# Taking the steps of a fused convolution and MLP in pairs: both first products, then both second products

## The chip, the cores and the metric

The kernel runs on one core of a Trainium2 chip. The metric is the device time of one execution in microseconds; the time of the kernel before is the median of three runs. The profile is that of one further execution.

## The reference

```
w = softmax(weight)                       # 8 heads x 7 taps
x_unf = x_pad[:, idx, :]                  # the last 7 rows of the sequence, zeros ahead of it
out = einsum('hk,bskhg->bshg', w, x_unf)  # causal convolution; 192 channels, 24 to a head
h = out.reshape(B * S, D) @ w_in          # 32768 x 192 by 192 x 2048
g = h * (1.0 / (1.0 + np.exp(-1.702 * h)))
return g @ w_out                          # by 2048 x 192
```

Everything is float32, with B = 8, S = 4096 and D = 192.

## The kernel before

**Tiling.** The work is cut into 32 "big" pieces of 1024 tokens of x (two batches of 512 tokens), and each into two steps, an even and an odd one: 64 steps. Within a step, the first product (by `w_in`, L463) gives eight tiles of hidden values, 128 partitions x 1024 each; ScalarE's gelu (L479) writes them to `g`; the second product (by `w_out`, `product2`, L553, and `quarters`, L569) gives the 192 outputs of the step's tokens.

**Fewer multiplications.** Both products are done in a scheme that saves block products and pays with sums of blocks. For the first, `terms` runs through 21 terms, each a call of `product1`: four pairs of matmuls, one half of the array's rows reading `f` and the other `crossed`. Their results are gathered in four PSUM tiles (`slots[0]` to `slots[2]`, called x, y and z in turn, and `sums`), and in five SBUF tiles `kept` (k15, k20, k19, k18, k16), by copies on ScalarE and additions on VectorE. For the second, `g` holds the four plain tiles B11, B12, B21, B22 and three sums, T1 = B12 - B11, T2 = B22 - T1 and T4 = T2 - B21; T3 = B22 - B12 takes B12's place. Each is in two halves of 128 x 1024 (u = 0, 1), and `sum_g` (L489) makes one half of one sum on VectorE.

**Steps.** The first two steps (`first_step`, `second_step`) use plain products, because the sums of weights aren't there yet. Then, for each step, `hidden` does the 21 terms, and `output` the five `product2` (p1, p2, p6, p5, p7) and the quarters. So TensorE alternates in each step between two shapes of matmul: 64 rows x 128 columns (L463) and 128 rows x 32 columns (L553, L569). Near its end, `hidden` calls `fetch`, which starts term 16 of the next step in a free slot, and `begin` copies the result to `sums`.

**What sets the order.** The schedule is written by hand: each engine runs its instructions in the order of the program, and the framework adds the waits on semaphores. Term 3 and term 19 near the end of `hidden` add to `sums` after k20's addition (L533) has read it. In `output`, T4 is read by the fourth column group of p5, and p2 reads B21.

**Work for the next x.** `prepare(big)` makes a list, `todo`, of VectorE instructions: three transposes of x, 21 taps of the convolution (L402, L404), eight sums of blocks, and DMAs that cross halves of `f` to the other partitions (`cross`). `work(us)` takes as many from the list as fit into the given time by fixed costs (0.76 for a tap, 0.7 for a transpose) and puts them at this place of VectorE's order. `need` takes all up to a label.

**Output.** `output` keeps partial sums u1, u2, p3, p4 in SBUF, adds to them on VectorE, transposes (`turn`, L587) into `osb`, and SP stores it.

The lines that set a step of `hidden` and its successors, where the change acts:

```
pe(sums, 1, 9, first=True)
pe(y, 15)
sum_g(0, T1)
work(1.1)
vec.tensor_add(k20, k20, sums)
...
sum_g(0, T2)
fetch()
pe(sums, 3, 19)
```

Of the kernel before, what the change touches and what calls it, by code (L numbers as in the profile page):

```python
# [8 lines left out]
F32 = mybir.dt.float32  # L9
U32 = mybir.dt.uint32  # L10
# [5 lines left out]
def kernel(  # L16
# [7 lines left out]
):  # L24

# [25 lines left out]
    P = 128  # L51
# [28 lines left out]
    u_pool = ctx.enter_context(tc.tile_pool(name="u", bufs=1))  # L80
    osb_pool = ctx.enter_context(tc.tile_pool(name="osb", bufs=2))
# [34 lines left out]
    NS = 7  # L116
    B11, B12, B21, B22, T1, T2, T4 = range(NS)
    T3 = B12
    g = consts.tile([P, NS, NK, T], F32)

# [44 lines left out]
    FREE = 10  # L165

# [6 lines left out]
    kept = [consts.tile([P, 2, TOK], F32, name=f"kept{i}") for i in range(5)]  # L173

# [10 lines left out]
    assert PIECE == CW * D and NW * 2 * PIECE == 3 * NK * T and 3 * PIECE <= NB * T  # L188
    raw = g[:, T1 : T4 + 1, :, :].rearrange("p s f t -> p (s f t)").bitcast(U32)
    raw = raw.rearrange("p (i n) -> p i n", i=NW)  # L190

    assert 2 * K * R <= NK * T and PIECE <= 2 * TOK and 3 * PIECE <= 2 * NJ * XW
    diag = g[:, B22, :, :].rearrange("p f t -> p (f t)")[:, 0 : 2 * K * R]
    diag = diag.rearrange("p (c k q) -> p c k q", c=2, k=K)

    def scratch(flat):
# [5 lines left out]
        [k.rearrange("p h n -> p (h n)")[:, 0:PIECE].bitcast(U32) for k in kept[0:3]],  # L202
# [4 lines left out]
    SET = (0, 1, 2, 0, 1, 3, 0, 1)  # L207
# [4 lines left out]
    ident = consts.tile([P, P], F32)  # L212
# [11 lines left out]
    for i in range(NW):  # L224
        piece = raw[:, i, :].rearrange("p (k f) -> p k f", k=NC)
        for h in range(2):
            nc.sync.dma_start(out=piece[halves[h], :, :], in_=w_in_v[i // 2, i % 2, h])


    sel = consts.tile([H, NC, P], F32)  # L230
# [13 lines left out]

    fold = consts.tile([P, R], F32)
# [6 lines left out]
    def words(i):  # L252
        w = raw[:, i % NW, :].rearrange("p (n w) -> p n w", w=2)
        return (w[:, :, 0], w[:, :, 1]) + tuple(sets[SET[i]])

# [67 lines left out]
    def load_w_out(i):  # L323
        nc.sync.dma_start(
            out=raw[:, i, :].rearrange("p (c d) -> p c d", c=CW),
            in_=w_out_v[:, i * CW : (i + 1) * CW, :],
        )
# [149 lines left out]
    def gelu(b, u, src):  # L477
        j = NK // 2 * u
        act.activation(  # L479
            g[:, b, j : j + NK // 2, :].rearrange("p f t -> p (f t)"),  # L480
            src.rearrange("p h n -> p (h n)"),
            AF.Gelu_apprx_sigmoid,
        )

    def sum_g(u, dst):
        j = NK // 2 * u
        v = [g[:, b, j : j + NK // 2, :] for b in range(NS)]
        a, b = {T1: (B12, B11), T2: (B22, T1), T3: (B22, B12), T4: (T2, B21)}[dst]
        vec.tensor_sub(v[dst], v[a], v[b])  # L489
# [6 lines left out]
    def hidden(s, x, z, y, work, fetch):  # L496

        k15, k16, k19, k18, k20 = kept

        def pe(slot, *ts, first=False):  # L500
            terms(s, slot, *ts, first=first)

        pe(sums, 12)
        act.copy(k15, sums)
        pe(x, 5, 17)
        gelu(B11, 0, x)
        pe(z, 7, first=True)
        pe(sums, 0)
        act.copy(k16, sums)
        work(1.5)  # L510
        pe(y, 6, 14, first=True)
        vec.tensor_sub(x, z, k15)
        work(2.6)
        pe(sums, 13)
        act.copy(k19, sums)  # L515
        pe(x, 2)
        act.copy(k18, x)
        pe(z, 11)
        pe(sums, 20, 10)
        vec.tensor_sub(k15, y, k19)  # L520
        gelu(B12, 0, sums)
        pe(x, 4)
        act.copy(k20, x)
        vec.tensor_sub(k19, z, k19)
        work(1.1)
        gelu(B22, 1, k19)
        gelu(B22, 0, k15)
        pe(y, 8)
        pe(sums, 1, 9, first=True)
        pe(y, 15)  # L530
        sum_g(0, T1)
        work(1.1)
        vec.tensor_add(k20, k20, sums)  # L533
        vec.tensor_sub(k16, y, k16)
        gelu(B11, 1, k20)
        pe(x, 18)
        gelu(B21, 1, x)
        gelu(B21, 0, k16)
        sum_g(0, T2)
        fetch()  # L540
        pe(sums, 3, 19)
        work(0.7)
        vec.tensor_add(k18, k18, sums)  # L543
        gelu(B12, 1, k18)
        work(1.1)

    def product2(slot, bank, ab, last, first=True):

        dst = slot[:, bank, 0:T]
        tiles = [(c, *ab, c) for c in range(NC)] + [(NC, *last)]  # L550
        for j in range(NK):
            for l, a, b, c in tiles:
                nc.tensor.matmul(  # L553
                    dst[l * Q : (l + 1) * Q, :],
                    w_out_s[:, a, j, c * Q : (c + 1) * Q],
                    g[:, b, j, :],
                    start=(first and j == 0),
                    stop=(j == NK - 1),
                    skip_group_check=True,
                )  # L560
        return dst[0 : NC * Q, :], dst[NC * Q :, :]

    def quarters(slot, bank, a, b, c):

        dst = [slot[l * Q : (l + 1) * Q, bank, 0:T] for l in range(4)]
        for i in range(NK // 4):
            for l in range(4):
# [4 lines left out]
                    g[:, b, j, :],  # L572
# [6 lines left out]
    class Out:  # L579


        def __init__(self, s):
            self.s = s
            self.osb = osb_pool.tile([NC * Q, 2, T // Q, 2 * Q], F32, name="osb")
# [24 lines left out]
    def output(s, ra, rb, work, between=None):  # L609

        out = Out(s)
        u1, u2, p3, p4 = (
            u_pool.tile([NC * Q, T], F32, name=f"u{i}") for i in range(4)
        )

        p1, p3c = product2(ra, 0, (A11, B11), (S4, B22, 0))
        act.copy(u1, p1)
        act.copy(chunk(p3, 0), p3c)
        sum_g(1, T1)
        sum_g(1, T2)  # L620
        sum_g(1, T4)
        sum_g(0, T4)
        p2, p3c = product2(rb, 0, (A12, B21), (S4, B22, 1))
# [3 lines left out]
        sum_g(0, T3)  # L627
        sum_g(1, T3)
        p6, p3c = product2(ra, 1, (S2, T2), (S4, B22, 2))
        act.copy(chunk(p3, 2), p3c)  # L630
        vec.tensor_add(u2, u1, p6)
        work(4.2)
        if between:
            between()
        p5, p4c = product2(rb, 1, (S1, T1), (A22, T4, 0))
        q = quarters(rb, 0, A22, T4, 2)
# [4 lines left out]
        out.turn(0, 1, p3)  # L641
        for l in (0, 1, 3):
            vec.tensor_add(chunk(p4, 2), chunk(p4, 2), q[l])
        work(1.5)
        p7, p4c = product2(ra, 0, (S3, T3), (A22, T4, 1))
# [42 lines left out]
    def first_step():  # L688
# [53 lines left out]
        gelu(B11, 0, slots[0])  # L742
        gelu(B12, 0, sums)
        for m, n, slot, b in quarters[2:]:
            plain(0, 0, m, n, slot)
            gelu(b, 0, slot)
# [11 lines left out]
        split_piece(5)  # L758
        split_rest(5)
        round_w_out(0)  # L760
        round_w_out(1)
        split_piece(6)
        split_piece(7)
        for m, n, slot, b in quarters:
            plain(0, 1, m, n, slot)
            gelu(b, 1, slot)
        split_rest(6)
        split_rest(7)
        round_w_out(2)
        round_w_out(3)  # L770


        todo.extend(prepare(1))
        todo.extend(("", 0.42, lambda i=i: sums_w_in(i)) for i in range(FREE))
        out = Out(0)
        c22 = u_pool.tile([NC * Q, T], F32, name="u0")
        quarter = [(0, 0), (0, 1), (1, 0)]
        for k in range(2):
            for i, (m, n) in enumerate(quarter):
                c, c22c = product2(  # L780
                    slots[i % 2],
# [5 lines left out]
                if k == 1:  # L787
                    work((6.0, 0.7, 2.3)[i])
                    out.turn(m, n, c)
                    act.copy(chunk(c22, i), c22c)  # L790
                    if i == 0:
                        sums_w_out()
        out.turn(1, 1, c22)
        out.store()

    def second_step(fetch):

        quarters = [
            (0, 0, slots[2], B11), (1, 0, sums, B21), (1, 1, slots[0], B22), (0, 1, slots[1], B12)
        ]  # L800
        for u in range(2):
            for i, (m, n, slot, b) in enumerate(quarters):
                plain(1, u, m, n, slot)
                gelu(b, u, slot)
                if u == 1 and i < 2:
                    sum_g(0, (T1, T2)[i])
                work(2.5)
        todo.extend(("", 0.42, lambda i=i: sums_w_in(i)) for i in range(FREE, len(SUMS_W)))
        todo.append(("sums", 0.0, lambda: None))
        todo.extend(prepare(2))  # L810
        output(1, slots[0], slots[1], work, fetch)
        need("all 1")
        cross(1, 1)
        need("sums")

    first_step()
    y, x, z = slots[0], slots[2], slots[1]
# [6 lines left out]
    def begin(slot):  # L824
        act.copy(sums, slot)

    def fetch_2():
        fetch(2, x)
        begin(x)

    second_step(fetch_2)
    for s in range(2, N_ST):
        more = s + 1 < N_ST
        hidden(s, x, z, y, work, lambda: fetch(s + 1, z) if more else None)
        give(s)
        if more:
            begin(z)
# [37 lines left out]
```

## Time and profile before

| | |
|---|---|
| runs (us) | 2381.71, 2382.17, 2382.23 |
| median | 2382.17 |
| span of the profiled execution | 2380.2 |
| TensorE matmuls / VectorE / ScalarE busy | 2370.6 / 2038.6 / 1055.7 |
| granted TensorE clock | 1.00 |
| repeat of a step in the middle | 36.60 |
| VectorE busy in two steps of 36.60 (985.37 to 1058.57) | 34.07 and 29.41 |

In a line of groups stand the source line, the engine, the operation, what it writes and reads, partitions x elements and type, and the count; then the busy time in us and the mean of one in ns; then the engine's idle time just ahead of such instructions, and what ended most of it. In a timeline, the first column is the start in us from the start of the span, the second the time from the first start to the last end of the instructions merged into that line, and a bracket gives idle time before it and who ended it. "PE" is the matmul, "PEld" the load of its weights, "DVE" is VectorE and "ACT" ScalarE. An fp32 matmul shows as two instructions, so that the page counts twice as many as the program has.

### The profile page before, as it was taken

Reading aid. Unit: us, or ns where it says so; the run is one execution under the profiler, and the core shown is the slowest. Engines: PE = TensorE matmul, PEld = TensorE weight load, DVE = VectorE, ACT = ScalarE, POOL = GpSimd, SP = SyncE. Lnnn points to the kernel's source line nnn. Section 1 sums busy time; section 2 is a strip of 40 time slices with the busy share of each in tenths; the row PEclk is TensorE's granted clock in tenths of the full one; section 3 lists DMA queues with packets and bytes.
Section 4 is the critical chain, followed back from the end, with each engine's and each line's share of the span. In section 5 each row is a group of like instructions: output and inputs, shape, how many; then the busy total and the mean of one; then the engine's idle time right before and its main releaser. Section 6 shows DMA issues by size and latency. Waiting matters only on the chain.

```text
span 2380.2 us, 71629 instructions
## 1 busy us (share of the span) xinstructions
PE 2370.6 (100%) x32602; PEld 1749.3 (73%) x32602; DVE 2038.6 (86%) x2853; ACT 1055.7 (44%) x1369; POOL 9.1 (0%) x30
## 2 busy tenths in 40 slices
PE   9999999999999999999999999999999999999998
PEld 7777777777777777777777777777777777777776
DVE  8898988888888889888898888898888988889865
ACT  6345344344453443444534434445344344453443
POOL 1000000000000000000000000000000000000000
PEclk9999999999999999999999999999999999999999
DMA  7322323223233132331232321323313233123120
GB/s 164 72 50 56 66 52 66 49 42 68 50 68 59 30 68 56 63 65 36 55 68 51 66 51 40 69 50 67 59 30 68 58 61 66 39 53 68 25 42 15
DMA packets 195823, 135.89 MB, mean 57 GB/s; under 512 B 110752, under 2 KB 186016, under 8 KB 193536
## 3 DMA queue, kind: packets, MB, share of 16 engines
q1 hardware_dynamic: 194912, 131.06, 28.1%
q8 instruction: 255, 4.18, 0.7%
q14 instruction: 48, 0.39, 0.1%
q10 hardware_dynamic: 560, 0.13, 0.0%
q0 software_dynamic: 48, 0.13, 0.0%
HBM read 53.15 MB, written 25.17 MB: 33 GB/s over the span
## 4 chain that ended last, share of the span: by engine, by line
PE 99%; ACT 0%; DVE 0%; POOL 0%; issue 0%; POOLq 0%
PE slot L553 47%; PE slot L463 28%; PE sums L463 21%; PE slot L569 2%; PE slot L675 1%; ACT g L479 0%; POOL sel L235 0%; PE sums L366 0%; PE slot L377 0%; DVE w_in_s L295 0%; DVE f L291 0%; ACT xin L281 0%; ACT xin L280 0%; ACT f L281 0%; ACT f L282 0%
## 5 line engine op out<-in xcount | busy, mean ns | idle before, releaser
L553 PE MATMUL slot<-g,w_out_s 128*32 128x256 f32 x20544 | 1133.5, 379 | 0.0
L553 PEld LDWEIGHTS slot<-g,w_out_s 128*32 128x32 f32 x20544 | 661.0, 110 | 451.2 <-issue 20.9
L463 PE MATMUL slot<-f,w_in_s 64*128 64x256 f32 x3120 | 724.7, 376 | 1.6 <-DVE w_in_s L295 1.6
L463 PE MATMUL slot<-crossed,w_in_s 64*128 64x256 f32 x3120 | 724.7, 376 | 0.0
L489 DVE TENSOR_TENSOR g<-g 128x1024 f32<-128x1024 f32 x504 | 602.7, 1216 | 81.8 <-ACT g L479 76.7
L463 PEld LDWEIGHTS slot<-f,w_in_s 64*128 64x128 f32 x3120 | 583.1, 187 | 36.8 <-ACT kept L278 2.0
L463 PEld LDWEIGHTS slot<-crossed,w_in_s 64*128 64x128 f32 x3120 | 583.1, 187 | 34.9 <-issue 0.4
L463 PE MATMUL sums<-f,w_in_s 64*128 64x256 f32 x2280 | 558.9, 379 | 0.0
L463 PE MATMUL sums<-crossed,w_in_s 64*128 64x256 f32 x2280 | 558.9, 379 | 0.0
L463 PEld LDWEIGHTS sums<-crossed,w_in_s 64*128 64x128 f32 x2280 | 421.4, 187 | 36.7 <-issue 12.8
L463 PEld LDWEIGHTS sums<-f,w_in_s 64*128 64x128 f32 x2280 | 421.4, 187 | 36.7 <-issue 12.8
L404 DVE SCALAR_TENSOR_TENSOR f<-xt,cw,f 128x512 f32<-128x512 f32 (+1 forms) x570 | 423.1, 742 | 14.4
L479 ACT ACTIVATE g<-kept 128x1024 f32<-128x1024 f32 x310 | 320.9, 1058 | 141.6 <-DVE kept L543 82.5
L479 ACT ACTIVATE g<-slot 128x1024 f32<-128x1024 f32 x136 | 138.3, 1017 | 49.2 <-PE slot L463 49.2
L637 ACT COPY u<-slot 32x256 f32<-32x256 f32 x63 | 23.1, 367 | 248.5 <-PE slot L569 248.5
L520 DVE TENSOR_TENSOR kept<-slot,kept 128x1024 f32<-128x1024 f32 x62 | 75.7, 1221 | 63.7 <-ACT kept L515 63.7
L533 DVE TENSOR_TENSOR kept<-kept,sums 128x1024 f32<-128x1024 f32 x62 | 75.7, 1221 | 55.9 <-PE sums L463 55.9
L587 DVE STREAM_TRANSPOSE osb<-u 96x256 f32<-96x256 f32 x253 | 111.2, 439 | 7.1 <-ACT u L790 0.4
L479 ACT ACTIVATE g<-sums 128x1024 f32<-128x1024 f32 x66 | 67.5, 1023 | 97.8 <-PE sums L463 97.8
L630 ACT COPY u<-slot 32x256 f32<-32x256 f32 x63 | 23.0, 364 | 194.5 <-PE slot L553 194.5
L515 ACT COPY kept<-sums 128x1024 f32<-128x1024 f32 x62 | 62.7, 1012 | 97.8 <-PE sums L463 97.8
L543 DVE TENSOR_TENSOR kept<-kept,sums 128x1024 f32<-128x1024 f32 x62 | 75.7, 1221 | 27.2 <-PE sums L463 24.3
(116 smaller groups left out, 1353.3 us busy)
## 6 DMA issues: line engine op xcount, KB each, us to landing
xin<-in_x_dram SPq DMA_DIRECT2D x240, 180.0 KB, 5.0
crossed<-f SPq DMA_DIRECT2D x31, 832.0 KB, 5.7
out_dram<-osb SPq DMA_DIRECT2D x382, 64.0 KB, 1.9
crossed<-f SPq DMA_DIRECT2D x31, 448.0 KB, 3.8
crossed<-f SPq DMA_DIRECT2D x31, 256.0 KB, 2.9
crossed<-f SPq DMA_DIRECT2D x31, 128.0 KB, 2.2
g<-in_moe_w_in_dram SPq DMA_DIRECT2D x8, 384.0 KB, 9.8
g<-in_moe_w_out_dram SPq DMA_DIRECT2D x4, 768.0 KB, 4.8
```

The source lines that it names most:

```text
L404: vec.scalar_tensor_tensor(out=dst, in0=src, scalar=tap, in1=dst, op0=ALU.mult, op1=ALU.add)
L463: nc.tensor.matmul(slot[:, h, j * T : (j + 1) * T], w_in_s[halves[h], a, j * P : (j + 1) * P], (f if h == o else crossed)[halves[h], b, :] ...
L479: act.activation(g[:, b, j : j + NK // 2, :].rearrange("p f t -> p (f t)"), src.rearrange("p h n -> p (h n)"), AF.Gelu_apprx_sigmoid,)
L489: vec.tensor_sub(v[dst], v[a], v[b])
L515: act.copy(k19, sums)
L520: vec.tensor_sub(k15, y, k19)
L533: vec.tensor_add(k20, k20, sums)
L543: vec.tensor_add(k18, k18, sums)
L553: nc.tensor.matmul(dst[l * Q : (l + 1) * Q, :], w_out_s[:, a, j, c * Q : (c + 1) * Q], g[:, b, j, :], start=(first and j == 0), stop=(j == ...
L569: nc.tensor.matmul(dst[l], w_out_s[:, a, j, c * Q : (c + 1) * Q], g[:, b, j, :], start=(i == 0), stop=(i == NK // 4 - 1), skip_group_check ...
L587: vec.transpose(self.osb[:, n, :, m * Q : (m + 1) * Q], src.rearrange("p (j t) -> p j t", t=Q),)
L675: nc.tensor.matmul(slots[c][halves[h], 0 if h == o else 1, n * T : (n + 1) * T], diag[halves[o], c - 1, k, :], xts[0][halves[o], c, n, Q - ...
```

## The change

The steps of a big piece are run as a pair: `hidden` of the even step, `hidden` of the odd one, then `output` of the even step and `output` of the odd one. What has to live longer, or in another place, follows from that:

- `g` holds the four plain tiles twice, one set for each step of a pair. T4 is written into B21's place.
- The five kept tiles become one tile, `room`. T1 and T2 of the step whose output is being made lie in k15, k20, k19 and k18, and u1, u2, p3, p4 in k16.
- In the odd `hidden`, T1 and T2 (half 0) of the even step are made; the odd step's follow in the even `output`, behind the additions to p4. Term 7 comes first in the odd `hidden`, since its slot is free. The even `hidden` copies the fetched slot to y, which serves the odd step as `sums`.
- In `output` T3 comes ahead of T4, and the amounts of `work` change.
- The first two steps are merged (`first_steps`): their first products all come ahead of their second ones. The loaded words of the weights, `ident`, `sel`, `fold` and `diag` get other places.

```diff
-    g = consts.tile([P, NS, NK, T], F32)
+    T3, T4 = B12, B21
+    g = consts.tile([P, 2, NU, 4, NK // NU, T], F32)
+    room = consts.tile([P, 5, 2 * TOK], F32)
+    k15, k20, k19, k18, k16 = (room[:, i, :].rearrange("p (h n) -> p h n", h=2) for i in range(5))
+    us = [room[0 : NC * Q, 4, i * T : (i + 1) * T] for i in range(4)]
+    def half(s, b, u):
+        if b in (T1, T2):
+            return room[:, 2 * (b - T1) + u, :].rearrange("p (f t) -> p f t", t=T)
+        return g[:, s % 2, u, b, :, :]
...
-    def hidden(s, x, z, y, work, fetch):
+    def hidden(s, x, z, y, sums, work, fetch):
+        if second:
+            pe(z, 7, first=True)
         pe(sums, 12)
         act.copy(k15, sums)
         pe(x, 5, 17)
-        gelu(B11, 0, x)
-        pe(z, 7, first=True)
+        gelu(s, B11, 0, x)
+        if not second:
+            pe(z, 7, first=True)
         pe(sums, 0)
         act.copy(k16, sums)
-        work(1.5)
+        work(3.2 if second else 1.5)
...
         pe(y, 15)
-        sum_g(0, T1)
+        if second:
+            sum_1(s - 1, 0)
+        else:
+            work(1.2)
         work(1.1)
         vec.tensor_add(k20, k20, sums)
         vec.tensor_sub(k16, y, k16)
-        gelu(B11, 1, k20)
+        gelu(s, B11, 1, k20)
         pe(x, 18)
-        gelu(B21, 1, x)
-        gelu(B21, 0, k16)
-        sum_g(0, T2)
+        gelu(s, B21, 1, x)
         fetch()
+        if not second:
+            act.copy(y, z)
+        gelu(s, B21, 0, k16)
+        if second:
+            sum_2(s - 1, 0)
+        else:
+            work(1.2)
         pe(sums, 3, 19)
...
     def output(s, ra, rb, work, between=None):
-        sum_g(1, T1)
-        sum_g(1, T2)
-        sum_g(1, T4)
-        sum_g(0, T4)
+        sum_1(s, 1)
+        sum_2(s, 1)
+        sum_3(s, 0)
+        sum_3(s, 1)
+        work(0.7)
...
         out.turn(0, 0, u2)
-        sum_g(0, T3)
-        sum_g(1, T3)
+        sum_4(s, 0)
+        sum_4(s, 1)
...
-        work(4.2)
+        work(3.2)
...
-        out.turn(0, 1, p3)
         for l in (0, 1, 3):
             vec.tensor_add(chunk(p4, 2), chunk(p4, 2), q[l])
-        work(1.5)
+        out.turn(0, 1, p3)
+        if s % 2:
+            work(1.5)
+        else:
+            sum_1(s + 1, 0)
+            sum_2(s + 1, 0)
...
-    for s in range(2, N_ST):
-        more = s + 1 < N_ST
-        hidden(s, x, z, y, work, lambda: fetch(s + 1, z) if more else None)
-        give(s)
-        if more:
-            begin(z)
-        if s % 2 and (s + 3) // 2 < N_BIG:
-            todo.extend(prepare((s + 3) // 2))
-        output(s, y, x, work)
-        if s % 2 and more:
-            need(f"all {(s + 1) // 2}")
-            cross((s + 1) // 2, 1)
-        x, z = z, x
+    for big in range(1, N_BIG):
+        s = 2 * big
+        more = big + 1 < N_BIG
+        hidden(s, x, z, y, sums, work, lambda: fetch(s + 1, z))
+        give(s)
+        x, z, y, sums = z, x, sums, y
+        hidden(s + 1, x, z, y, sums, work, lambda: fetch(s + 2, z) if more else None)
+        if more:
+            act.copy(sums, z)
+        output(s, y, x, work)
+        if more:
+            need(f"all {big + 1}")
+            cross(big + 1, 1)
+        if big + 2 < N_BIG:
+            todo.extend(prepare(big + 2))
+        output(s + 1, x, y, work)
+        x, y, z = z, x, y
```

More of the change, by code (lines that the diff above doesn't have):

```diff
@@ L79 @@
     f_pool = ctx.enter_context(tc.tile_pool(name="f", bufs=2))
-    u_pool = ctx.enter_context(tc.tile_pool(name="u", bufs=1))
-    osb_pool = ctx.enter_context(tc.tile_pool(name="osb", bufs=2))
     psum = ctx.enter_context(tc.tile_pool(name="psum", bufs=1, space=bass.MemoryType.PSUM))
@@ L112 @@
     sums = psum.tile([P, 2, TOK], F32, name="sums")
-    NS = 7
-    B11, B12, B21, B22, T1, T2, T4 = range(NS)
-    T3 = B12
-    g = consts.tile([P, NS, NK, T], F32)
+    B11, B12, B21, B22, T1, T2 = range(6)
+    T3, T4 = B12, B21
[3 more added lines that the diff above has]
+    us = [room[0 : NC * Q, 4, i * T : (i + 1) * T] for i in range(4)]
+    osbs = consts.tile([P, 2, 2 * TOK], F32)
+    def half(s, b, u):
+        if b in (T1, T2):
+            return room[:, 2 * (b - T1) + u, :].rearrange("p (f t) -> p f t", t=T)
+        return g[:, s % 2, u, b, :, :]
     NB = 13
@@ L163 @@
     ]
-    FREE = 10
     TERMS = [
@@ L170 @@
     ]
-    kept = [consts.tile([P, 2, TOK], F32, name=f"kept{i}") for i in range(5)]
+    NS = 7
     A11, A12, A21, A22, S1, S2, S4 = range(NS)
@@ L187 @@
     PIECE = NC * UW
[L188 to L194, printed above, removed]
+    assert PIECE == CW * D and 3 * PIECE <= NB * T and 3 * PIECE <= 2 * NJ * XW
+    flat_room = room.rearrange("p i n -> p (i n)")
+    flat_osb = osbs.rearrange("p i n -> p (i n)")
+    later = [g[:, 1, u, :, :, :].rearrange("p b f t -> p (b f t)") for u in range(NU)]
+    at = [(flat_osb, 0), (flat_room, 3 * PIECE), (later[1], 2 * TOK), (later[1], 2 * TOK + 2 * PIECE)]
+    assert 5 * PIECE + R <= 4 * 2 * TOK and 2 * TOK + 4 * PIECE <= 4 * NK // NU * T
+    raw = [t[:, i : i + 2 * PIECE].bitcast(U32) for t, i in at]
+    diag = later[0][:, 0 : 2 * K * R].rearrange("p (c k q) -> p c k q", c=2, k=K)
+    sel = flat_osb[0:H, 2 * PIECE : 2 * PIECE + NC * P].rearrange("i (c q) -> i c q", c=NC)
+    ident = flat_osb[:, 2 * PIECE + NC * P :]
+    assert 2 * PIECE + (NC + 1) * P == 4 * TOK
+    fold = flat_room[:, 5 * PIECE : 5 * PIECE + R]
     def scratch(flat):
@@ L201 @@
         scratch(tmp),
-        [k.rearrange("p h n -> p (h n)")[:, 0:PIECE].bitcast(U32) for k in kept[0:3]],
+        scratch(flat_room),
         None,
@@ L205 @@
     ]
-    SET = (0, 1, 2, 0, 1, 3, 0, 1)
+    SET = (0, 1, 2, 0, 1, 3, 1, 3)
     w8 = consts.tile([H, K], F32)
     act.dma_start(out=w8, in_=weight)
-    ident = consts.tile([P, P], F32)
     make_identity(nc, ident)
@@ L224 @@
     for i in range(NW):
-        piece = raw[:, i, :].rearrange("p (k f) -> p k f", k=NC)
+        piece = raw[i].rearrange("p (k f) -> p k f", k=NC)
         for h in range(2):
             nc.sync.dma_start(out=piece[halves[h], :, :], in_=w_in_v[i // 2, i % 2, h])
-    sel = consts.tile([H, NC, P], F32)
     nc.gpsimd.memset(sel, 1.0)
@@ L243 @@
             )
-    fold = consts.tile([P, R], F32)
     nc.gpsimd.tensor_add(fold, ident[:, 0:R], ident[:, R:P])
@@ L252, in words @@
     def words(i):
-        w = raw[:, i % NW, :].rearrange("p (n w) -> p n w", w=2)
+        w = raw[i % NW].rearrange("p (n w) -> p n w", w=2)
         return (w[:, :, 0], w[:, :, 1]) + tuple(sets[SET[i]])
@@ L324, in load_w_out @@
         nc.sync.dma_start(
-            out=raw[:, i, :].rearrange("p (c d) -> p c d", c=CW),
+            out=raw[i].rearrange("p (c d) -> p c d", c=CW),
             in_=w_out_v[:, i * CW : (i + 1) * CW, :],
@@ L475, in terms, with gelu @@
             first = False
-    def gelu(b, u, src):
-        j = NK // 2 * u
+    def gelu(s, b, u, src):
         act.activation(
-            g[:, b, j : j + NK // 2, :].rearrange("p f t -> p (f t)"),
+            half(s, b, u).rearrange("p f t -> p (f t)"),
             src.rearrange("p h n -> p (h n)"),
@@ L483, in gelu, with sum_g, sum_1, sum_2 @@
         )
[L485 to L489, printed above, removed]
+    def sum_g(s, u, dst, terms):
+        vec.tensor_sub(half(s, dst, u), half(s, terms[0], u), half(s, terms[1], u))
+    def sum_1(s, u):
+        sum_g(s, u, T1, (B12, B11))
+    def sum_2(s, u):
+        sum_g(s, u, T2, (B22, T1))
+    def sum_3(s, u):
+        sum_g(s, u, T3, (B22, B12))
+    def sum_4(s, u):
+        sum_g(s, u, T4, (T2, B21))
     def plain(s, u, m, n, slot, ks=range(NC), first=0):
@@ L494, in plain @@
             product1(slot, NC * (2 * u + m) + k, 2 * k + n, s, k == first)
-    def hidden(s, x, z, y, work, fetch):
-        k15, k16, k19, k18, k20 = kept
+    def hidden(s, x, z, y, sums, work, fetch):
+        second = s % 2
         def pe(slot, *ts, first=False):
             terms(s, slot, *ts, first=first)
+        if second:
+            pe(z, 7, first=True)
         pe(sums, 12)
@@ L520, in hidden @@
         vec.tensor_sub(k15, y, k19)
-        gelu(B12, 0, sums)
+        gelu(s, B12, 0, sums)
         pe(x, 4)
@@ L525, in hidden @@
         work(1.1)
-        gelu(B22, 1, k19)
-        gelu(B22, 0, k15)
+        gelu(s, B22, 1, k19)
+        gelu(s, B22, 0, k15)
         pe(y, 8)
@@ L543, in hidden, with product2 @@
         vec.tensor_add(k18, k18, sums)
-        gelu(B12, 1, k18)
-        work(1.1)
-    def product2(slot, bank, ab, last, first=True):
+        gelu(s, B12, 1, k18)
+    def product2(s, slot, bank, ab, last, first=True):
         dst = slot[:, bank, 0:T]
@@ L555, in product2 @@
                     w_out_s[:, a, j, c * Q : (c + 1) * Q],
-                    g[:, b, j, :],
+                    half(s, b, j // (NK // NU))[:, j % (NK // NU), :],
                     start=(first and j == 0),
@@ L561, in product2, with quarters @@
         return dst[0 : NC * Q, :], dst[NC * Q :, :]
-    def quarters(slot, bank, a, b, c):
+    def quarters(s, slot, bank, a, b, c):
         dst = [slot[l * Q : (l + 1) * Q, bank, 0:T] for l in range(4)]
@@ L571, in quarters @@
                     w_out_s[:, a, j, c * Q : (c + 1) * Q],
-                    g[:, b, j, :],
+                    half(s, b, j // (NK // NU))[:, j % (NK // NU), :],
                     start=(i == 0),
@@ L583, in __init__ @@
             self.s = s
-            self.osb = osb_pool.tile([NC * Q, 2, T // Q, 2 * Q], F32, name="osb")
+            self.osb = osbs[0 : NC * Q, s % 2, :].rearrange(
+                "q (n j e) -> q n j e", n=2, e=2 * Q
+            )
         def turn(self, m, n, src):
@@ L611, in output @@
         out = Out(s)
[L612 to L616, printed above, removed]
+        u1, u2, p3, p4 = us
+        p1, p3c = product2(s, ra, 0, (A11, B11), (S4, B22, 0))
         act.copy(u1, p1)
         act.copy(chunk(p3, 0), p3c)
-        sum_g(1, T1)
-        sum_g(1, T2)
-        sum_g(1, T4)
-        sum_g(0, T4)
-        p2, p3c = product2(rb, 0, (A12, B21), (S4, B22, 1))
+        sum_1(s, 1)
[3 more added lines that the diff above has]
+        work(0.7)
+        p2, p3c = product2(s, rb, 0, (A12, B21), (S4, B22, 1))
         act.copy(chunk(p3, 1), p3c)
@@ L626, in output @@
         out.turn(0, 0, u2)
-        sum_g(0, T3)
-        sum_g(1, T3)
-        p6, p3c = product2(ra, 1, (S2, T2), (S4, B22, 2))
+        sum_4(s, 0)
+        sum_4(s, 1)
+        p6, p3c = product2(s, ra, 1, (S2, T2), (S4, B22, 2))
         act.copy(chunk(p3, 2), p3c)
         vec.tensor_add(u2, u1, p6)
-        work(4.2)
+        work(3.2)
         if between:
             between()
-        p5, p4c = product2(rb, 1, (S1, T1), (A22, T4, 0))
-        q = quarters(rb, 0, A22, T4, 2)
+        p5, p4c = product2(s, rb, 1, (S1, T1), (A22, T4, 0))
+        q = quarters(s, rb, 0, A22, T4, 2)
         act.copy(chunk(p4, 0), p4c)
@@ L640, in output @@
         vec.tensor_add(p3, u1, p3)
-        out.turn(0, 1, p3)
         for l in (0, 1, 3):
             vec.tensor_add(chunk(p4, 2), chunk(p4, 2), q[l])
-        work(1.5)
-        p7, p4c = product2(ra, 0, (S3, T3), (A22, T4, 1))
+        out.turn(0, 1, p3)
[4 more added lines that the diff above has]
+            sum_2(s + 1, 0)
+        p7, p4c = product2(s, ra, 0, (S3, T3), (A22, T4, 1))
         act.copy(chunk(p4, 1), p4c)
@@ L686, in take_conv, with first_steps @@
         (act.copy if engine is act else vec.tensor_copy)(dst, slots[c][:, bank, :])
-    def first_step():
+    def first_steps(fetch):
         first, second = slice(0, 1), slice(1, 2)
@@ L741, in first_step @@
         plain(0, 0, 0, 1, sums, (2, 0), 1)
-        gelu(B11, 0, slots[0])
-        gelu(B12, 0, sums)
+        gelu(0, B11, 0, slots[0])
+        gelu(0, B12, 0, sums)
         for m, n, slot, b in quarters[2:]:
             plain(0, 0, m, n, slot)
-            gelu(b, 0, slot)
+            gelu(0, b, 0, slot)
         cross(0, 1, C11, C21, nc.gpsimd)
@@ L757, in first_step, with piece_5, piece_6, piece_7 @@
         load_x(1)
[L758 to L774, printed above, removed]
+        def piece_5():
+            split_piece(5)
+            split_rest(5)
+            round_w_out(0)
+        def piece_6():
+            split_piece(6)
+            split_rest(6)
+            round_w_out(1)
+        def piece_7():
+            split_piece(7)
+            split_rest(7)
+            round_w_out(2)
+        def prepare_1():
+            round_w_out(3)
+            todo.extend(prepare(1))
+            todo.extend(("", 0.42, lambda i=i: sums_w_in(i)) for i in range(len(SUMS_W)))
+            todo.append(("sums", 0.0, lambda: None))
+        between = [None, piece_5, None, piece_6, None, piece_7, None, prepare_1]
+        for s, u in ((0, 1), (1, 0), (1, 1)):
+            for m, n, slot, b in quarters:
+                plain(s, u, m, n, slot)
+                gelu(s, b, u, slot)
+                if between:
+                    (between.pop(0) or (lambda: None))()
+                else:
+                    work(2.5)
         out = Out(0)
-        c22 = u_pool.tile([NC * Q, T], F32, name="u0")
+        c22 = us[0]
         quarter = [(0, 0), (0, 1), (1, 0)]
+        sum_1(1, 0)
+        sum_2(1, 0)
+        work(6.5)
         for k in range(2):
@@ L780, in first_step @@
                 c, c22c = product2(
+                    0,
                     slots[i % 2],
@@ L787, in first_step @@
                 if k == 1:
-                    work((6.0, 0.7, 2.3)[i])
+                    if i == 0:
+                        sums_w_out()
                     out.turn(m, n, c)
                     act.copy(chunk(c22, i), c22c)
-                    if i == 0:
-                        sums_w_out()
+                    work(2.5)
         out.turn(1, 1, c22)
         out.store()
[L796 to L811, printed above, removed]
         need("all 1")
         cross(1, 1)
+        todo.extend(prepare(2))
+        output(1, slots[1], slots[0], work, fetch)
         need("sums")
-    first_step()
-    y, x, z = slots[0], slots[2], slots[1]
     def fetch(s, slot):
@@ L822, in fetch @@
         terms(s, slot, 16, first=True)
-    def begin(slot):
-        act.copy(sums, slot)
     def fetch_2():
-        fetch(2, x)
-        begin(x)
-    second_step(fetch_2)
-    for s in range(2, N_ST):
-        more = s + 1 < N_ST
-        hidden(s, x, z, y, work, lambda: fetch(s + 1, z) if more else None)
+        fetch(2, slots[2])
+        act.copy(sums, slots[2])
+    first_steps(fetch_2)
+    x, y, z = slots[2], slots[1], slots[0]
+    for big in range(1, N_BIG):
+        s = 2 * big
+        more = big + 1 < N_BIG
+        hidden(s, x, z, y, sums, work, lambda: fetch(s + 1, z))
         give(s)
+        x, z, y, sums = z, x, sums, y
+        hidden(s + 1, x, z, y, sums, work, lambda: fetch(s + 2, z) if more else None)
         if more:
-            begin(z)
-        if s % 2 and (s + 3) // 2 < N_BIG:
-            todo.extend(prepare((s + 3) // 2))
+            act.copy(sums, z)
         output(s, y, x, work)
-        if s % 2 and more:
-            need(f"all {(s + 1) // 2}")
-            cross((s + 1) // 2, 1)
-        x, z = z, x
+        if more:
[5 more added lines that the diff above has]
+        x, y, z = z, x, y
 _INS = ['x', 'weight', 'moe_w_in', 'moe_w_out']
```

## The prediction

> **What bounds the kernel now.** I read the page first (engine shares and chain), then its groups, then the timelines of TensorE, VectorE and ScalarE over one step in the middle, and last the waits of the start.
>
> ```profile
> PE 2370.6 (100%) x32602; PEld 1749.3 (73%) x32602; DVE 2038.6 (86%) x2853; ACT 1055.7 (44%) x1369; POOL 9.1 (0%) x30
> ...
> PE 99%; ACT 0%; DVE 0%; POOL 0%; issue 0%; POOLq 0%
> ...
> L553 PE MATMUL slot<-g,w_out_s 128*32 128x256 f32 x20544 | 1133.5, 379 | 0.0
> ...
> L489 DVE TENSOR_TENSOR g<-g 128x1024 f32<-128x1024 f32 x504 | 602.7, 1216 | 81.8 <-ACT g L479 76.7
> ...
> L479 ACT ACTIVATE g<-kept 128x1024 f32<-128x1024 f32 x310 | 320.9, 1058 | 141.6 <-DVE kept L543 82.5
> ```
>
> TensorE is the chain, without a wait from about 45 us to the end. Busy time proves little for it, since matmuls overlap, so I look at the starts:
>
> ```profile
> 1002.22 0.38 PE L463 MATMUL sums<-crossed,w_in_s 64*128 64x256 f32 x1
> 1002.52 14.02 PE L553 MATMUL slot<-g,w_out_s 128*32 128x256 f32 x256
> 1016.36 1.05 PE L569 MATMUL slot<-g,w_out_s 128*32 128x256 f32 x16
> 1017.22 3.64 PE L553 MATMUL slot<-g,w_out_s 128*32 128x256 f32 x64
> 1020.79 0.48 PE L463 MATMUL sums<-crossed,w_in_s 64*128 64x256 f32 x1
> ...
> 1021.11 0.38 PE L463 MATMUL sums<-crossed,w_in_s 64*128 64x256 f32 x1
> ...
> 1037.30 0.38 PE L463 MATMUL sums<-crossed,w_in_s 64*128 64x256 f32 x1
> ```
>
> First products (L463) start in pairs every 0.216 us, so one term (four pairs) takes 0.863; one `product2` takes 3.49 (13.95 for four in the chain). Steps repeat every 36.60 us. Only the changes between the two kinds lie outside this beat: into L553 0.306 instead of 0.209, then 0.220 instead of 0.196 after the first group; back 0.309 instead of 0.196, then 0.313 instead of 0.209. That is 0.10+0.02+0.11+0.10 = 0.34 us for a round trip.
>
> **The skill.** The Trainium skill's page "TensorEngine Tiling (Array Packing)", Key Properties, says that a change of tiling mode drains the TensorE; the trace agrees, 0.34 us there and back between 64*128 and 128*32. "TensorE: Matmul & The Clock Gate", on queue depths, says that ACT and DVE work strictly in order while TensorE may draw weight loads ahead; here weights run one beat ahead, and a wait holds the load too. "VectorE: DVE Perf Modes", TRN2 errata, gives (N+151)/0.96 ns for an fp32 tensor_tensor: an estimate of 1224 ns for N = 1024, against 1216 measured. So a sum of `g` can't be had cheaper on VectorE.
>
> **Part 1, fewer round trips.** Before: 62 hidden steps, one for the first step, two for the second (its `fetch` splits it), 65. After: 31 pairs plus two, 33. 32 x 0.34 = 10.9 us gained. Matmuls (16,301 in both programs), VectorE and ScalarE instructions and DMAs are the same in number; nothing else is removed.
>
> **Part 2, the moved sum T1 in the second hidden step.** `sum_1(s-1, 0)` now writes the tile of k15, so it must wait for the gelu that reads k15, and k20's addition stands behind it on VectorE. TensorE's term 3 accumulates into `sums` and waits until that addition has read it.
>
> ```profile
> 1033.28 2.02 ACT L479 ACTIVATE g<-kept 128x1024 f32<-128x1024 f32 x2
> ...
> 1040.52 1.06 ACT L479 ACTIVATE g<-kept 128x1024 f32<-128x1024 f32 x1 [1.36 <-DVE kept L543]
> 1041.48 1.00 ACT L825 COPY sums<-slot 128x1024 f32<-128x1024 f32 x1
> ```
>
> ```profile
> 1017.87 0.42 DVE L638 TENSOR_TENSOR u<-u,slot 96x256 f32<-96x256 f32 x1
> ...
> 1034.99 1.22 DVE L533 TENSOR_TENSOR kept<-kept,sums 128x1024 f32<-128x1024 f32 x1 [1.24 <-PE sums L463]
> 1036.13 1.22 DVE L534 TENSOR_TENSOR kept<-slot,kept 128x1024 f32<-128x1024 f32 x1
> ...
> 1039.26 1.22 DVE L543 TENSOR_TENSOR kept<-kept,sums 128x1024 f32<-128x1024 f32 x1 [0.78 <-PE sums L463]
> 1041.61 3.75 DVE L489 TENSOR_TENSOR g<-g 128x1024 f32<-128x1024 f32 x3 [1.12 <-ACT g L479]
> ```
>
> The two gelus of k19 and k15 end at 1035.30. Put the new order on this clock: T1 starts at 1035.33; the addition of k20 (L533, at 1034.99 today) starts 1.14 later (the step from L533 to L534), 1036.47, and ends at 1037.69. Term 3 starts at 1037.30 today. What a late release costs TensorE is seen once, in the start:
>
> ```profile
> 38.10 0.96 DVE L295 SCALAR_TENSOR_TENSOR w_in_s<-f 128x768 f32<-128x768 f32 x1
> ```
>
> ```profile
> 39.20 0.45 PE L463 MATMUL slot<-f,w_in_s 64*128 64x256 f32 x1 [1.62 <-DVE w_in_s L295]
> 39.21 0.48 PE L463 MATMUL slot<-crossed,w_in_s 64*128 64x256 f32 x1
> ```
>
> VectorE ends at 39.06, the matmul starts 0.14 later, and the next pair after 0.285 instead of 0.21, 0.07 more. So the wait costs 0.39 + 0.14 + 0.07 = 0.60 us a pair. Bounds: 0.39 (the release free of charge) and 0.80. 31 pairs give 18.6; the last has no fetch ahead of term 3 (+0.86), and the first still has a convolution in the way (+0.8): 20.3 us.
>
> **Part 3, no mode change between the hidden steps of a pair.** The second step starts where the first ends, 1039.02 on this clock. Its `act.copy(k15)` stands on ScalarE behind the gelu of the first step's k18, in the place of today's copy of `sums` (L825): it ends at 1042.49. The term 0 that overwrites `sums` comes fifth, at 1039.02 + 4 x 0.863 = 1042.47. Release 0.02 late, plus 0.14 and 0.07: 0.23 us a pair, 7.1 us. Bounds 0 and 0.35 (the program has 187 more semaphore instructions on ScalarE, one just ahead of this copy; I count them at nothing elsewhere, ScalarE being idle 56%).
>
> **Part 4, VectorE between the two outputs.** In `output` of the even step, T1 and T2 of the odd step (half 0) stand behind the additions to p4, and halves 1, T3 twice and one transpose of x behind them, all ahead of T4, which the third tile column of p5 needs (T4 now lies in B21's place, so it can't come before p2 has read B21). Counted from the end of the quarters (1017.22), start to start as in the timeline of VectorE: addition to u1 0.65 (L638 at 1017.87), p3 and three p4 additions, turn at 2.86, T1 3.23, T2 4.49 (1.26 when it depends on the one before, as in the 3.75 of three), u1 and p7 at 5.63, the five small ones to 7.44 (0.34, 0.33, 0.36, 0.41, 0.37), T1 7.44, T2 8.70, T3 9.84 and 10.97, transpose 12.1, u2 12.8 (0.70), turn 13.25, T4 13.62, which ends at 14.80. TensorE wants it at four `product2` after the quarters, 13.96. Late by 0.84, with the release 0.98 us. Over those 14.80 us VectorE has no idle time to give back; before it, while p6 and p5 of the even step run, it has some 4 us free, because the list of work for the next x is empty by then. Bounds: 0.5 if the small ones pack better, 1.4 if they slip as far as u2's additions, which p2 waits for (6.38 against 6.98). 29 pairs have the transpose, the last two (no further x) some 0.25: 28.9 us.
>
> **Edits at nothing.** T1 and T2 in `room` and g twice: same sizes, same engines, and sums that went to g go to another tile. Output sums in k16's tile: the copy of k16 comes 4.3 us into the first hidden step, VectorE's tail of the output ends about 3.2 us into it. The copy into y is 1.01 us on ScalarE, hidden by the last two terms (1.73) and term 7. SP's queue: same DMAs; the crossing for the odd half moves behind the even output, a whole hidden step ahead of its reader; the even one (5.7 us to landing) has the second hidden step. POOL only sets zeros. In the start, VectorE's list is the same work in another order, and twelve more first products (10.4 us) stand ahead of the first second product, so the weights' rounding has more time; I take 0, within -2 and +4.
>
> **Sum.** -10.9 + 20.3 + 7.1 + 28.9 = +45.4 on the profiled span of 2380.2, so 2425.6; the runs' median lies 2.0 above this span: 2427.6 us.
>
> **Rivals.** (a) All three waits vanish (the order has slack that I misjudge, VectorE catches up in the 10 us a pair that it is idle: 63.5 busy of 73.2): then 2382.2 - 10.9 = 2371.3, faster. Against it: part 2 is a wait for one instruction whose end is in the trace. It decides where k20's addition ends before 1037.1. (b) Only the waits in the second hidden step are real, part 4 is not: 2399. For it: the chain of part 4 has 20 links, each of which may be 0.03 shorter. (c) VectorE's lateness spreads to p2 of the odd output and the hidden step after it: 0.5 us more a pair, 2443. (d) The change doesn't save mode changes, if `fetch` or the order of TensorE still alternates: the program's order shows both first products, then both second ones, so no; and a gain equal to the waits (no change) needs two of the three absent.
>
> **How the numbers follow.** Main case 0.71 (2410 to 2440), (b) 0.13, (c) 0.05, (a) 0.08, no change 0.03. Low ends of parts 2 to 4 (12.1 + 0 + 15) less 10.9 give 2398; high ends (26.5 + 10.9 + 41) less 10.9 give 2450. The range 2395 to 2448 leaves out (a), no change and the tails. About 0.2% is what a measurement of this kernel can tell from no change. Faster 0.08, same 0.03, slower 0.89.
>
> **What would show it.** Round trips: 33 entries from L463's successor to L553's; TensorE idle before term 3 of odd steps, put down to k20's addition, 0.4 to 0.8; before the fifth term, 0.1 to 0.3, put down to the copy of k15; in p5 of odd outputs, about 1, put down to T4. The pair takes 74.7 us instead of 73.2. Pairs of 72.9 us would prove me wrong.

## The result, and the profile after

The changed kernel takes 2426.56 us (median of six, 2425.47 to 2426.76), the kernel before 2381.95 (median of six): ratio 1.0186, 95% interval 1.0173 to 1.0199. It is slower by 44.6 us; the forecast was +45.4. The span of the profiled execution is 2424.7 us.

The page of the kernel after, the lines that answer to those shown of before:

```profile
PE 2391.2 (99%) x32602; PEld 1755.3 (72%) x32602; DVE 2018.8 (83%) x2853; ACT 1052.7 (43%) x1369; POOL 9.1 (0%) x30
...
PE 73%; DVE 15%; ACT 6%; issue 3%; DMA 2%; SPq 1%; POOL 0%; DVEq 0%; POOLq 0%; ACTq 0%
...
L472 PE MATMUL slot<-crossed,w_in_s 64*128 64x256 f32 x3940 | 904.9, 378 | 7.3 <-DVE room L557 7.3
...
L582 PE MATMUL slot<-g,w_out_s 128*32 128x256 f32 x9792 | 781.5, 379 | 9.0 <-DVE g L494 9.0
```

Counts are as before: 32,602 matmul records, 2853 VectorE and 1369 ScalarE instructions. But the chain, 99% TensorE before, now runs through VectorE and ScalarE as well. The idle times beside the matmuls (7.3 and 9.0 us) are too small to tell the loss, because the ends of the matmuls are modelled and cover part of the gaps. The waits of the weight loads tell more; here are those of the kernel after (total, times, longest):

```profile
PEld slot L582 <- DVE g L494: 18.5, 20, 1.0
PEld slot L472 <- DVE room L557: 15.7, 21, 1.5
PEld sums L582 <- DVE g L494: 10.2, 11, 1.3
...
PEld sums L472 <- DVE room L557: 6.7, 10, 0.7
PEld slot L472 <- ACT room L524: 5.5, 21, 0.3
...
PEld sums L472 <- ACT room L524: 2.6, 10, 0.3
```

Three causes, 31 waits each (20+11, 21+10, 21+10): T4 (L494), k20's addition (L557), the copy of k15 (L524). They are the three of the forecast. Their prices are read from the starts of matmuls, against the beat where nothing waits: 0.216 us from the start of one pair of first products to the start of the next.

**Term 3.** TensorE, VectorE and ScalarE of the kernel after, around the addition of k20 in an odd hidden step:

```profile
1036.78 0.38 PE L472 MATMUL slot<-crossed,w_in_s 64*128 64x256 f32 x1
1037.43 0.48 PE L472 MATMUL slot<-crossed,w_in_s 64*128 64x256 f32 x1 [0.27 <-DVE room L557]
1037.44 0.48 PE L472 MATMUL slot<-f,w_in_s 64*128 64x256 f32 x1
1037.75 0.38 PE L472 MATMUL slot<-crossed,w_in_s 64*128 64x256 f32 x1
```

```profile
1035.02 1.23 DVE L494 TENSOR_TENSOR room<-g 128x1024 f32<-128x1024 f32 x1 [3.44 <-ACT g L487]
1036.16 1.21 DVE L557 TENSOR_TENSOR room<-room,slot 128x1024 f32<-128x1024 f32 x1
```

```profile
1032.97 2.02 ACT L487 ACTIVATE g<-room 128x1024 f32<-128x1024 f32 x2
```

VectorE idles for 3.44 us with T1 at the head of its queue, until the gelu of k15 ends at 1034.99. Then T1 and, 1.14 later, the addition, which ends at 1037.37. From the start of one matmul pair to the next it is 0.65 us instead of 0.22, then 0.32 instead of 0.22: 0.44 + 0.10 = 0.54 us. Of the 0.44, 0.38 is the lateness of the addition and 0.06 the time from its end to the matmul (the release).

**The fifth term.** ScalarE, and the pairs of matmuls where the fifth term of the odd step begins:

```profile
1021.93 1.06 ACT L487 ACTIVATE g<-room 128x1024 f32<-128x1024 f32 x1 [0.38 <-DVE room L573]
1022.89 0.99 ACT L524 COPY room<-slot 128x1024 f32<-128x1024 f32 x1
```

```profile
1023.70 0.38 PE L472 MATMUL slot<-crossed,w_in_s 64*128 64x256 f32 x1
...
1023.94 0.48 PE L472 MATMUL slot<-crossed,w_in_s 64*128 64x256 f32 x1
...
1024.26 0.38 PE L472 MATMUL slot<-crossed,w_in_s 64*128 64x256 f32 x1
```

The copy of k15 stands behind the gelu of the even step's k18 and ends at 1023.89. The fifth term starts at 1023.94, only 0.02 late, but the next pair of matmuls again comes after 0.32 instead of 0.22: together 0.13 us.

**T4.** VectorE from the quarters of an even output to p5 of the odd one, and TensorE at p5:

```profile
1054.71 0.42 DVE L668 TENSOR_TENSOR room<-room,slot 96x256 f32<-96x256 f32 x1 [3.90 <-ACT room L667]
...
1057.34 1.18 DVE L494 TENSOR_TENSOR room<-g 128x1024 f32<-128x1024 f32 x1
...
1063.97 2.36 DVE L494 TENSOR_TENSOR g<-g 128x1024 f32<-128x1024 f32 x2
1066.25 0.77 DVE L396 STREAM_TRANSPOSE xt<-xin 128x576 f32<-128x576 f32 x1
...
1067.72 2.31 DVE L494 TENSOR_TENSOR g<-room,g 128x1024 f32<-128x1024 f32 x2
```

```profile
1054.06 3.64 PE L582 MATMUL sums<-g,w_out_s 128*32 128x256 f32 x64
...
1067.88 0.61 PE L582 MATMUL sums<-room,w_out_s 128*32 128x256 f32 x6
1068.95 0.40 PE L582 MATMUL sums<-g,w_out_s 128*32 128x256 f32 x1 [0.47 <-DVE g L494]
```

The quarters end at 1054.06 (counted, as in the prediction, to the start of the next product). T1 starts 3.28 us later (forecast 3.23), T4 13.66 (13.62). VectorE is 3.90 us idle just ahead of this stretch and has no gap within it. T4's first half ends at 1068.90, 14.84 after the quarters, and p5 begins at 1067.88, 13.82 after them: 1.02 us late. Of p5, the three matmuls that stand ahead of T4's first in the program have run (the x6: three column groups, two instructions each). T4's starts at 1068.95, and the next matmuls of the other three groups, which stand behind it in the program, at 1068.96.

### The profile page after: what moved, and what is told of

Read it like the earlier page. It is cut to its first block, busy times and chain, and to the rows that moved or that the text cites. A ratio compares the mean times of both kernels' runs of the same rounds, so it can differ in the third digit from the quotient of the medians.

```text
span 2424.7 us, 71778 instructions
## 1 busy us (share of the span) xinstructions
PE 2391.2 (99%) x32602; PEld 1755.3 (72%) x32602; DVE 2018.8 (83%) x2853; ACT 1052.7 (43%) x1369; POOL 9.1 (0%) x30
## 4 chain that ended last, share of the span: by engine, by line
PE 73%; DVE 15%; ACT 6%; issue 3%; DMA 2%; SPq 1%; POOL 0%; DVEq 0%; POOLq 0%; ACTq 0%
PE slot L472 30%; PE slot L582 20%; PE sums L472 11%; PE sums L582 9%; DVE room L494 4%; ACT g L487 4%; DVE g L494 3%; DMA out_dram<-osbs 2%; DVE osbs L618 2%; PE slot L598 2%; DVE room L557 1%; ACT room L544 1%; DVE room L672 1%; DVE xt L396 1%; SPq L633 1%
## 5 line engine op out<-in xcount | busy, mean ns | idle before, releaser
L472 PE MATMUL slot<-f,w_in_s 64*128 64x256 f32 x3940 | 905.1, 378 | 1.6 <-DVE w_in_s L304 1.6
L582 PE MATMUL slot<-g,w_out_s 128*32 128x256 f32 x9792 | 781.5, 379 | 9.0 <-DVE g L494 9.0
L582 PEld LDWEIGHTS slot<-g,w_out_s 128*32 128x32 f32 x9792 | 422.8, 110 | 227.6 <-DVE g L494 18.5
L582 PE MATMUL sums<-g,w_out_s 128*32 128x256 f32 x4704 | 385.6, 379 | 5.1 <-DVE g L494 5.1
L487 ACT ACTIVATE g<-room 128x1024 f32<-128x1024 f32 x310 | 321.3, 1059 | 132.6 <-DVE room L557 105.2
L472 PE MATMUL sums<-crossed,w_in_s 64*128 64x256 f32 x1460 | 360.6, 378 | 2.7 <-DVE room L557 2.7
L472 PE MATMUL sums<-f,w_in_s 64*128 64x256 f32 x1460 | 360.6, 378 | 0.0
L582 PE MATMUL slot<-room,w_out_s 128*32 128x256 f32 x4032 | 305.2, 379 | 0.0
L582 PEld LDWEIGHTS sums<-g,w_out_s 128*32 128x32 f32 x4704 | 205.0, 110 | 111.9 <-DVE g L494 10.2
L494 DVE TENSOR_TENSOR room<-g 128x1024 f32<-128x1024 f32 x126 | 151.2, 1200 | 106.1 <-ACT g L487 106.1
L494 DVE TENSOR_TENSOR room<-g,room 128x1024 f32<-128x1024 f32 x126 | 154.1, 1223 | 5.5
L494 DVE TENSOR_TENSOR g<-g 128x1024 f32<-128x1024 f32 x126 | 148.3, 1218 | 0.0
L494 DVE TENSOR_TENSOR g<-room,g 128x1024 f32<-128x1024 f32 x126 | 145.8, 1195 | 0.0
```

The costliest lines, as they stand in the source:

```text
L472: nc.tensor.matmul(slot[:, h, j * T : (j + 1) * T], w_in_s[halves[h], a, j * P : (j + 1) * P], (f if h == o else crossed)[halves[h], b, :] ...
L487: act.activation(half(s, b, u).rearrange("p f t -> p (f t)"), src.rearrange("p h n -> p (h n)"), AF.Gelu_apprx_sigmoid,)
L494: vec.tensor_sub(half(s, dst, u), half(s, terms[0], u), half(s, terms[1], u))
L582: nc.tensor.matmul(dst[l * Q : (l + 1) * Q, :], w_out_s[:, a, j, c * Q : (c + 1) * Q], half(s, b, j // (NK // NU))[:, j % (NK // NU), :], ...
```

## The experiments

All are the kernel after with an edit, but for the fourth, which is the kernel before with one. Times are medians; "before" in these runs was 2382.2. "The pair" is two hidden steps and two outputs; its parts are measured from the first matmul of one shape to the first of the other. In the kernel after, the two hidden steps take 37.13 us and the two outputs 37.48, together 74.61:

```profile
1002.23 0.48 PE L472 MATMUL sums<-f,w_in_s 64*128 64x256 f32 x1
...
1039.36 3.66 PE L582 MATMUL sums<-g,w_out_s 128*32 128x256 f32 x64
...
1076.84 0.48 PE L472 MATMUL slot<-f,w_in_s 64*128 64x256 f32 x1
```

**T1 behind k16's subtraction**

```diff
-        if second:
-            sum_1(s - 1, 0)
-        else:
+        if not second:
             work(1.2)
...
         if second:
+            sum_1(s - 1, 0)
             sum_2(s - 1, 0)
```

> The changed kernel, but in the odd hidden step T1 (half 0) stands behind k16's subtraction, just ahead of T2, so that k20's addition no longer stands behind a wait for the gelu of k15. Own theory (three separate waits, each from the order of one queue): TensorE's wait before term 3 goes (0.44 + 0.10 us in 29 pairs, 1.2 in the first, 1.4 in the last, 18.4 us in all), the other two stay: 2408 us. Rival, that VectorE has too little time in the paired stretch, so that the wait only moves: 2420 or more, with a new wait of TensorE in the even output.

Measured: 2407.43 us (ratio 1.0107, 1.0090 to 1.0124), 19.1 less. The hidden pair shortens from 37.13 to 36.59 us, the outputs stay at 37.48, and no wait of TensorE on k20's addition is left. The wait hung on T1's place in VectorE's queue.

**T3 and the transpose behind T4 in the odd output**

```diff
-        sum_3(s, 0)
-        sum_3(s, 1)
-        work(0.7)
+        if s % 2 == 0:
+            sum_3(s, 0)
+            sum_3(s, 1)
+            work(0.7)
...
         sum_4(s, 1)
+        if s % 2:
+            sum_3(s, 0)
+            sum_3(s, 1)
+            work(0.7)
```

> The changed kernel, but in the odd output both halves of T3 and the transpose of x stand behind T4. Own theory: T4 is ready at about 12.8 us after the quarters, before p5 asks at 13.8, and T3 still 2 us before p7; the wait of 1.08 us in p5 goes in 29 pairs: 2395 us. Rival, VectorE short of time: T3 comes late for p7, or the hidden step behind waits, and 2415 or more.

Measured: 2427.32 us (1.0174 to 1.0204 of before), nothing gained; my expectation missed by 32 us. The wait in p5 did go. Waits of TensorE in this kernel:

```profile
PE slot L472 <- DVE slot L533: 8.9, 29, 0.3
PE slot L472 <- DVE room L557: 7.3, 21, 1.1
PE slot L472 <- ACT room L524: 5.8, 19, 0.3
...
```

No line names L494 any more. In its place stand 29 waits on L533, the subtraction of k15 from term 7's result early in the even hidden step, and the waits on k15's copy are longer. The two outputs shorten from 37.48 to 36.40 us, but the two hidden steps grow from 37.13 to 38.29. VectorE's timeline of the same kernel (the quarters of the odd output end at 1072.14) shows why:

```profile
1065.08 0.42 DVE L656 TENSOR_TENSOR room<-room,sums 96x256 f32<-96x256 f32 x1 [1.07 <-ACT room L655]
...
1070.41 0.77 DVE L396 STREAM_TRANSPOSE xt<-xin 128x576 f32<-128x576 f32 x1
...
1073.23 1.54 DVE L413 SCALAR_TENSOR_TENSOR f<-xt,cw,f 128x512 f32<-128x512 f32 x2
1074.69 0.41 DVE L673 TENSOR_TENSOR room<-room,sums 96x256 f32<-96x256 f32 x1
```

The addition to u1 (L673), possible 0.65 us after the quarters, starts 2.55 after them: T3, the transposes and the taps stand ahead of it. The lateness is handed on: in the pair that begins at 1001.02, VectorE has no idle time above 0.1 us until 1031.27, so it is late at L533 and late at the addition to k18, which the copy of k15 waits for by way of a gelu. Part of it comes from the new order itself, in which the addition of p2 (L656) leaves VectorE idle for 1.07 us within the full stretch. The rival (VectorE short of time) was right on this stretch, though not on the wait of term 3.

**Both edits**

> Both edits of the two runs ahead of it. Own theory: the waits add up, 18.4 + 31.3 us go, 2377 us, below the kernel before by about 5, with the wait for k15's copy (0.13 us a pair) left. Rival, VectorE short of time: 2400 or more. Rival, that fewer round trips between the two shapes of matmul save nothing: not below 2382.

Measured: 2408.7 us (1.0096 to 1.0126). The gain of the first edit stays, the second gives nothing here either (outputs 36.40 us, hidden steps 37.75 instead of 36.59). So the expectation of 2377 failed with the second edit, and the point on round trips stayed open.

**The kernel before with more round trips**

```diff
-        hidden(s, x, z, y, work, lambda: fetch(s + 1, z) if more else None)
+        hidden(s, x, z, y, work, lambda: None)
         give(s)
-        if more:
-            begin(z)
+        def fetch_next():
+            fetch(s + 1, z)
+            begin(z)
...
-        output(s, y, x, work)
+        output(s, y, x, work, fetch_next if more else None)
```

> The kernel before, but the fetch of each next step stands in the middle of output (ahead of p5) instead of inside hidden: 61 more round trips between the two shapes of matmul, the same instructions otherwise. Own theory: 61 x 0.34 = 20.7 us more, 2402.7 us. Rival, that a round trip is free: 2382 us.

Measured: 2402.99 us (1.0072 to 1.0102), 20.8 more, 0.34 us for each of 61 round trips. A step takes 36.94 us instead of 36.60, and TensorE's matmuls wait for no other engine outside the start. So the 32 that the change saves are worth 10.9 us.

**A tile of its own for T1**

```diff
+    own = consts.tile([P, 2 * TOK], F32)
     def half(s, b, u):
+        if b == T1 and u == 0:
+            return own.rearrange("p (f t) -> p f t", t=T)
```

> The changed kernel in its own order, but T1 (half 0) has a tile of its own instead of k15's place. If the wait before term 3 comes from the shared place (T1 must wait for the gelu that reads k15, and k20's addition stands behind it), it goes: 2408 us, as where T1 stood later. If it comes from T1 standing there at all, as 1.2 us of VectorE's time, no more than a third goes: 2420 or more.

Measured: 2407.04 us (1.0091 to 1.0119), as with T1 moved. Order or place, either alone removes this wait: T1's 1.2 us of VectorE time there cost nothing, the sharing of k15's place did.

**The list of work filled early**

To the two first edits this adds (step 1, the odd one of the two first steps, keeps its old amounts):

```diff
+        if big + 2 < N_BIG:
+            todo.extend(prepare(big + 2))
         output(s, y, x, work)
...
-        if big + 2 < N_BIG:
-            todo.extend(prepare(big + 2))
...
-        work(3.2)
+        work(1.5 if s % 2 and s > 1 else 3.2)
...
         if s % 2:
             sum_3(s, 0)
             sum_3(s, 1)
-            work(0.7)
+            if s == 1:
+                work(0.7)
```

> T1 later and T3 behind T4 in the odd output, and besides the list of work for the next x is filled ahead of the even output, where VectorE is idle for 3.9 us, and the odd output takes less of it (no transpose ahead of p2, 1.5 instead of 3.2 behind p6). The theory as corrected (the wait in p5 is a local shortage of VectorE from the quarters of the even output to the next hidden step, and moving T3 alone handed it on): no lateness is left at the end of the odd output, 31 us less than with T1 later alone, 2377 us. Rival, that pairing leaves too little time whatever stands where: 2395 or more.

Measured: 2375.25 us (0.9959 to 0.9982), faster than both kernels. The outputs of a pair now take 36.40 us instead of 37.48, and the hidden steps stay at 36.59. So the wait in p5 was worth 1.08 us a pair; against T1 moved alone, 32.2 us are gone.

**And the copy of k15 ahead of k18's gelu**

```diff
         act.copy(k15, sums)
+        if second:
+            gelu(s - 1, B12, 1, k18)
...
-        gelu(s, B12, 1, k18)
+        if second:
+            gelu(s, B12, 1, k18)
```

> The same as with the list filled early, and besides the copy of k15 in the odd hidden step stands ahead of the gelu of the even step's k18 on ScalarE. Own theory: the last wait (0.13 us in 31 pairs, 4.0 us) goes, 2373 us, which is the kernel before less the 10.8 us of saved round trips. Rival: the gelu of k18 and what stands behind it come late instead, and k16's copy holds term 13: 2376 or more.

Measured: 2371.1 us (0.9941 to 0.9966), the fastest of all. Hidden steps 36.46, outputs 36.40, together 72.86: two steps of before (73.20) less one round trip. All waits of TensorE's matmuls for other engines in this kernel lie in the start:

```profile
PE slot L472 <- DVE w_in_s L304: 1.6, 1, 1.6
PE sums L375 <- POOL osbs masks.py:199: 1.4, 1, 1.4
PE slot L386 <- POOL bias L259: 0.5, 1, 0.5
```

**The list early, but T3 ahead of T4**

T1 moved and the list filled early as above, with T3 where the change has it and no transpose between T3 and p2's addition. The odd output takes 1.5 instead of 3.2 from the list behind p6, as above.

> T1 later and the list filled early, but T3 stays ahead of T4 in the odd output (without the transpose). By the chain of VectorE, T4 ends 0.70 us earlier, at 14.1 after the quarters, against 13.8 asked: about 0.6 us of wait a pair are left of 1.08, 2393 us. Rival, that the transpose and the taps are the whole of it: 2377.

Measured: 2388.18 us (1.0016 to 1.0036). The outputs of a pair take 36.82 us, 0.42 more than without any wait. The next product after the quarters, and T4:

```profile
1038.29 1.48 PE L581 MATMUL sums<-g,w_out_s 128*32 128x256 f32 x24
```

```profile
1051.29 2.31 DVE L494 TENSOR_TENSOR g<-room,g 128x1024 f32<-128x1024 f32 x2
```

T4 starts 13.00 us after the quarters instead of 13.66. It is 0.66 us earlier, and the wait is 0.66 us shorter (0.42 of 1.08): here the price fell with T4's lateness, one to one. My expectation was 5 us too slow, because I put what is left at 0.6.

## Why the prediction was right, point by point

- **Round trips**, 10.9 us gained by forecast. Right: 0.34 us each by the added 61, and the fastest version comes out at 2382.2 - 11.1.
- **Term 3**, 0.60 us a pair, 20.3 us in all. Measured 0.54 in the pair shown, 19.1 us by the first experiment. The lateness was right (0.38, forecast 0.39). The release, which I had taken from the start, was too large (0.06, forecast 0.14), and the loss of the next pair of matmuls too small (0.10, forecast 0.07). The cause, T1 waiting for k15's place with the addition behind it, is shown twice, by order and by place.
- **Fifth term** (k15's copy behind k18's gelu), 7.1 us. Measured 4.15 us between the last two steps of the series (2375.25 to 2371.1), 0.13 a pair. Right in place, but 0.23 was too large, again by the release: the term starts 0.02 late (forecast 0.16), and the next pair of matmuls loses 0.10 (forecast 0.07).
- **T4 in p5**, 28.9 us. Measured 1.08 us a pair instead of 0.98, 32.2 us by the experiment. The chain of VectorE was right to about 0.1 us at each link, 0.04 at T4. The error is in when T4 is asked for: I had taken `product2` as 3.49 us, from durations; by its starts it is 3.46 (1002.52 to 1016.36 for four), so that p5 begins 13.82 us after the quarters and not 13.96. T4 is then 1.02 late (forecast 0.84), and the release took 0.06 (forecast 0.14).
- **Sum.** Between the runs' medians, 19.1 + 4.15 + 32.2 is the distance from the kernel after to the fastest version, so that these three less 10.9 must give about the measured 44.6, and only the 10.9 is tested by it. Added up pair by pair in the traces instead, the waits come to 18.4, 4.0 and 32.7 us; less 10.9 that is 44.2, against 44.6 measured. The edits priced at nothing (places, output sums in k16's tile, DMAs, the copy into y) leave little to explain: with the three waits gone and these edits in, the kernel lies 11.1 us below before.
- **Luck.** The forecast of the total missed by 0.8 us, but its terms by 1.2 and 3.0 one way and 3.3 the other. That they cancel is luck; that there are three waits, where they stand and what causes them is not.
- **Rival (a)**, all waits absent, 2371.3, did not come true for the change, but is the time of the last version (2371.1). It needed idle time of VectorE to be usable. Moving work by hand used some of it: of the 3.90 us ahead of the quarters' additions, 0.60 are left in the last version. I had said that VectorE had some 4 us free in the even output; what I had not drawn from it is that the cure lay there.
- **What I got wrong on the way** was the second experiment: I took the wait in p5 for one of order alone. VectorE was short of time from the quarters of the even output into the next hidden step, and another order handed the lateness on. Whether that order would have done with its 1.07 us of idle time filled was not tested.

## What to carry to other kernels

Where one engine has no idle time, read each moved instruction of the others by what stands behind it in its queue: an instruction with an early start by its data can wait for the place that it writes. Before a wait is mended by reordering, count the engine's work over the whole stretch: here it was full, reordering within it gained nothing, and moving work out of it did. And price gains of changing less often (0.34 us here) against waits of 0.1 to 1 us that each pairing can add.

## What the runs showed of the hardware that was not expected

When one of four column groups had to wait, the other three did not run ahead: after their first matmuls of p5 (x6 at 1067.88) nothing started until 1068.95. Their next matmuls stand behind T4's in the program, so this is what starting in the program's order gives; no run tests another order. The cost, 1.08 us, was that of the late group: T4's matmul started 1.06 us behind the beat, and the group's next instruction after 0.24 us instead of 0.22.

A late release cost the pairs of 64-row matmuls 0.10 us beyond its own delay in all 62 cases of the kernel after at term 3 and the fifth term (0.32 us to the next pair of matmuls instead of 0.22), the same as after each of its 33 changes to this shape. In the start it was less, 0.07 (0.29 instead of 0.22). So a start only 0.02 us late cost 0.13.
